# Interleaving the forward and inverse FFT stages of neighbouring channel chunks

## Chip, cores, metric

Each run used one core of one Trainium2 chip. The experiments were spread over three chips (e1 to e6, e7 to e10, e11 and e12), each time with the kernel before run beside them in the same rounds. The metric is device microseconds of one execution; a time is the median of several runs. Every ratio below is the mean time of one kernel's fast runs over the mean of the fast runs of the kernel before in the same rounds, so it is not quite the ratio of the medians.

## The reference

The kernel computes two independent things and puts them side by side in the output: (A) a dilated sliding-window attention over 2048 positions, and (B) an S4 state-space layer, which builds a convolution kernel K per channel and convolves the input u with it by FFT. Only the second half of (B) matters here:

```python
Kf = rfft(pad(K))             # 640 channels, length 2048 padded to 4096
Uf = rfft(pad(u))
y  = irfft(Uf * Kf)[:2048]    # to bfloat16
y  = y + u * Dskip
```

## The kernel before

The program has three stages: tables and K on VectorE (to 405 us), the FFT part (405 to 622 us), and attention (622 to 836 us). The FFT part treats 640 channels in five chunks of 128. Each FFT is two matmul steps. Forward: f1 (with the constant BD1) and f2 (with Tsb). Then VectorE multiplies the spectra (six products, "prod"). Inverse: ia (with EA) and ib (with HB). Every step ends in a tile in PSUM, the memory that the matmuls write (a one-bank tile is 128x512 float32 in these traces), and is copied out ("evacuated") by ScalarE or VectorE.

```python
def fft_chunk(...):                       # cut to its order
    for sig in range(2):                  # K, then U
        for jp in range(8):               # f1: 16 one-bank tiles
            ps = psp.tile([128, 2, 64, 4], f32, tag="bank")
            ...                           # 4 matmuls
            ev(A1[...], ps)
    for b0 in range(0, 32, 2):            # f2: 16 one-bank tiles
        ...                               # 8 matmuls, lhsT=Tsb, rhs=A1
        ev(S[...], ps)
    # prod: Yr = Kr*Ur - Ki*Ui (3 ops), Yi = Kr*Ui + Ki*Ur (3 ops), on VectorE
    for jp in range(8):                   # ia: 8 tiles, lhsT=Y
        ...
        ev(Z[...], ps)
    for lb in range(4):                   # ib: 4 tiles, lhsT=HB, rhs=Z
        ...
        ev(ysb[...], ps)
    ud = u * Dskip; ud = ud + ysb         # VectorE
    for g in range(4):                    # output
        (nc.sync if g % 2 == 0 else nc.scalar).dma_start(out=dst[g, ...], in_=ud[...])

# constants
nc.gpsimd.memset(Tsb[:], 0.0)             # then two loads of Tsb
nc.gpsimd.memset(HB[:], 0.0)              # then four loads of HB
...
ev = Evac(nc, "ad")                       # a = ScalarE, d = VectorE, in turn
for c in range(NCH):
    fft_chunk(tc, pools, C, c, ...)
```

A1, S, Y and Z each have one buffer; PSUM has eight one-bank buffers. A scheduler decides the final order on each engine, close to the program's.

## Time and profile before

| | before |
|---|---|
| time, median of 6 first runs | 837.46 us |
| FFT part: f2 of chunk 0 starts | 446.9 us |
| products of chunks 0 to 4 start | 457.3, 491.9, 526.1, 560.3, 594.4 us |
| attention's first load issued | 622.0 us |
| attention, to the end of the span | 214.0 us |

The distance between the starts of the products of neighbouring chunks (the "pitch") is the measure of the FFT loop: 34.3 us on average here.

First the page's busy rows of the kernel before: each digit is the busy share of one fortieth of the span in tenths; PEclk is the granted TensorE clock in tenths.

```profile
PE   4100000801702603504514768667728989378895
DVE  0899899999999999995113666676623076998670
ACT  1444200100200200200112334243214545202322
PEclk9999999855855855755756778898778999668998
```

The FFT part is slices 20 to 30. No engine is busy throughout, so something serial bounds it. The waits view of the kernel before for 404 to 640 us names it (columns: who waited on whom; total us, times, longest):

```profile
PE ps_ia L283 <- DVE Yf L272: 27.6, 5, 5.5
...
PE ps_f L261 <- DMA Tsb<-c_T: 20.3, 1, 20.3
...
PE ps_f L261 <- ACT A L232: 13.2, 4, 3.4
```

TensorE waits 5.5 us per chunk for the real half of the products, 20.3 us once for the load of Tsb, and about 3.3 us per chunk for the last evacuation of A1. The timeline of POOL in the kernel before shows where the late Tsb comes from (start, length, instruction):

```profile
407.05 10.38 POOL L213 MEMSET Tsb<- 128x12288 bf16 x1
417.33 13.79 POOL L218 MEMSET HB<- 128x16384 bf16 x1
431.03 2.21 POOL L215 DMA_DIRECT2D Tsb<-c_T  x1
433.21 2.19 POOL L216 DMA_DIRECT2D Tsb<-c_T  x1
```

The two memsets stand one after the other before the loads are issued. The ScalarE timeline of the kernel before shows where the A1 wait comes from:

```profile
474.99 2.54 ACT L232 CAST A<-ps_f 128x512 bf16<-128x512 f32 x5 [0.61 <-PE ps_f L252]
477.05 3.43 ACTq L299 DMA_DIRECT2D out_dram<-ud  x2
480.52 1.56 ACT L232 CAST A<-ps_f 128x512 bf16<-128x512 f32 x3 [2.99 <-DVE A L234]
```

ScalarE spends 3.43 us issuing two output DMAs; three A1 evacuations of the next chunk stand behind it. Finally two steady chunks in the windows view (busy us of PE, weight loads, DVE, ACT, POOL, then clock, DMA share, GB/s):

```profile
492.00:526.00 34.00, 24.00 (x448) 22.40 (x448) 23.38 (x30) 12.61 (x22) 0.00 (x0) 0.85 0.16 17
526.00:560.00 34.00, 23.98 (x448) 22.25 (x448) 23.36 (x30) 12.61 (x22) 0.00 (x0) 0.85 0.16 17
```

### The profile page before, as it was taken

Reading aid. Unit: us, or ns where it says so; the run is one execution under the profiler, and the core shown is the slowest. Engines: PE = TensorE matmul, PEld = TensorE weight load, DVE = VectorE, ACT = ScalarE, POOL = GpSimd, SP = SyncE. Lnnn points to the kernel's source line nnn. Section 1 sums busy time; section 2 is a strip of 40 time slices with the busy share of each in tenths; the row PEclk is TensorE's granted clock in tenths of the full one; section 3 lists DMA queues with packets and bytes.
Section 4 is the critical chain, followed back from the end, with each engine's and each line's share of the span. In section 5 each row is a group of like instructions: output and inputs, shape, how many; then the busy total and the mean of one; then the engine's idle time right before and its main releaser. Section 6 shows DMA issues by size and latency. Waiting matters only on the chain.

```text
span 836.0 us, 14737 instructions
## 1 busy us (share of the span) xinstructions
PE 394.8 (47%) x6720; PEld 296.6 (35%) x6720; DVE 597.6 (71%) x567; ACT 192.3 (23%) x327; POOL 39.4 (5%) x33
## 2 busy tenths in 40 slices
PE   4100000801702603504514768667728989378895
PEld 2000000701602503404414657656615466133534
DVE  0899899999999999995113666676623076998670
ACT  1444200100200200200112334243214545202322
POOL 0000000000000000000583000000000000000000
PEclk9999999855855855755756778898778999668998
DMA  4000000000000000000799012021049200000101
GB/s 84 1 0 0 0 0 0 3 0 0 3 0 1 2 0 1 2 0 2 109 58 97 12 17 28 2 27 19 9 82 302 45 2 5 1 0 1 64 1 65
DMA packets 96077, 21.86 MB, mean 26 GB/s; under 512 B 89488, under 2 KB 95888, under 8 KB 95888
## 3 DMA queue, kind: packets, MB, share of 16 engines
q0 software_dynamic: 29184, 2.82, 13.4%
q1 hardware_dynamic: 35552, 9.59, 6.0%
q10 hardware_dynamic: 31280, 8.52, 5.1%
q8 instruction: 52, 0.85, 0.4%
q14 instruction: 9, 0.07, 0.0%
HBM read 18.45 MB, written 5.24 MB: 28 GB/s over the span
## 4 chain that ended last, share of the span: by engine, by line
DVE 49%; PE 30%; DMA 7%; issue 4%; POOL 3%; ACT 3%; ACTq 2%; POOLq 0%; SPq 0%; DVEq 0%
DVE krtmp L139 6%; DVE krtmp L136 5%; DVE Ytab L140 4%; DVE Ytab L137 4%; DVE Ytab L135 4%; DVE Ytab L138 4%; PE ps_o L420 4%; PE ps_op L432 3%; PE ps_qk L354 3%; DVE chsq L123 3%; PE ps_k L169 2%; PE ps_ia L284 2%; PE ps_v L370 2%; DMA wsb<-in_A_wqkv_dram 2%; DVE Xtab L140 2%
## 5 line engine op out<-in xcount | busy, mean ns | idle before, releaser
L168 PE MATMUL ps_k<-Ytab,Xtab 128*32 128x64 bf16 x640 | 50.8, 331 | 260.3 <-DVE Ytab L137 143.6
L168 PEld LDWEIGHTS <-Xtab 128*32 128x32 bf16 x640 | 43.1, 160 | 261.4 <-issue 261.4
L176 ACT CAST Kall<-ps_k 128x512 bf16<-128x512 f32 x20 | 11.8, 588 | 292.2 <-PE ps_k L175 292.2
L384 DVE TENSOR_TENSOR prod<-qT,kT 128x5120 bf16<-128x5120 bf16 x16 | 44.3, 2821 | 37.1 <-ACT qT L362 33.8
L169 PE MATMUL ps_k<-Ytab,Xtab 128*32 128x64 bf16 x640 | 50.2, 327 | 29.5 <-DVE Ytab L140 29.5
L169 PEld LDWEIGHTS <-Xtab 128*32 128x32 bf16 x640 | 44.1, 162 | 33.6 <-DVE Ytab L140 30.8
L261 PE MATMUL ps_f<-A,Tsb 128*128 128x128 bf16 x160 | 39.1, 244 | 33.5 <-DMA Tsb<-c_T 20.3
L418 DVE TENSOR_TENSOR prod<-v,attn 128x2560 bf16<-128x2560 bf16 x32 | 45.9, 1488 | 7.4 <-PE ps_o L420 7.1
L283 PE MATMUL ps_ia<-EA,Yf 128*32 128x256 bf16 x320 | 37.0, 370 | 27.6 <-DVE Yf L272 27.6
L234 DVE CAST A<-ps_f 128x512 bf16<-128x512 f32 x40 | 25.0, 680 | 34.2 <-ACT A L232 25.3
L420 PE MATMUL ps_o<-prod,ident 128*128 128x512 bf16 x160 | 44.1, 410 | 6.5 <-DVE prod L418 5.7
L234 DVE CAST S<-ps_f 128x512 bf16<-128x512 f32 x40 | 25.4, 683 | 24.6 <-PE ps_f L264 24.4
L262 PE MATMUL ps_f<-A,Tsb 128*128 128x128 bf16 x160 | 39.1, 244 | 0.0
L264 PE MATMUL ps_f<-A,Tsb 128*128 128x128 bf16 x160 | 39.0, 244 | 0.0
L263 PE MATMUL ps_f<-A,Tsb 128*128 128x128 bf16 x160 | 39.0, 244 | 0.0
L174 PE MATMUL ps_k<-Ytab,Xtab 64*32 64x64 bf16 x640 | 38.2, 289 | 0.0
L175 PE MATMUL ps_k<-Ytab,Xtab 64*32 64x64 bf16 x640 | 37.8, 286 | 0.0
L432 PE MATMUL ps_op<-wo,o 32*128 32x320 bf16 x640 | 36.8, 298 | 1.8 <-ACT ob L437 1.6
L283 PEld LDWEIGHTS <-Yf 128*32 128x32 bf16 x320 | 23.9, 163 | 30.3 <-DVE Yf L272 28.4
L135 DVE TENSOR_TENSOR Ytab<-Ytab,gY 128x192 bf16<-128x192 bf16 (+4 forms) x25 | 32.3, 1291 | 2.2 <-ACT Ytab L154 2.2
L232 ACT CAST S<-ps_f 128x512 bf16<-128x512 f32 x40 | 23.5, 587 | 43.0 <-PE ps_f L264 43.0
L139 DVE TENSOR_TENSOR krtmp<-Ytab,gY 128x192 bf16<-128x192 bf16 (+4 forms) x25 | 32.4, 1298 | 0.9
(123 smaller groups left out, 1103.2 us busy)
## 6 DMA issues: line engine op xcount, KB each, us to landing
wsb<-in_A_wqkv_dram SPq DMA_DIRECT2D x2, 800.0 KB, 20.9
wo<-in_A_wo_dram ACTq DMA_DIRECT2D x2, 800.0 KB, 17.6
wo<-in_A_wo_dram SPq DMA_DIRECT2D x2, 800.0 KB, 24.8
Tsb<-c_T POOLq DMA_DIRECT2D x2, 768.0 KB, 12.4
Usb<-in_B_u_dram ACTq DMA_DIRECT2D x2, 640.0 KB, 12.4
Usb<-in_B_u_dram SPq DMA_DIRECT2D x2, 640.0 KB, 14.0
out_dram<-ud SPq DMA_DIRECT2D x10, 128.0 KB, 5.2
out_dram<-ud ACTq DMA_DIRECT2D x10, 128.0 KB, 6.5
```

The lines of the kernel that those rows point to most:

```text
L135: V.tensor_tensor(out=Or, in0=Yr, in1=gr, op=A.mult)
L136: V.tensor_tensor(out=t, in0=Yi, in1=gi, op=A.mult)
L139: V.tensor_tensor(out=t, in0=Yr, in1=gi, op=A.mult)
L140: V.tensor_tensor(out=Oi, in0=Oi, in1=t, op=(A.subtract if conj else A.add))
L168: nc.tensor.matmul(o, lhsT=Xtab[:, 0, :, colA], rhs=Ytab[:, 0, :, colA], start=(jj == 0 and dd == 0), stop=False, tile_position=(0, 32 * g ...
L169: nc.tensor.matmul(o, lhsT=Xtab[:, 1, :, colA], rhs=Ytab[:, 1, :, colA], start=False, stop=False, tile_position=(0, 32 * g), skip_group_ch ...
L234: self.nc.vector.tensor_copy(out=out, in_=in_)
L283: MM(o, lhsT=Y[:, :, 0, 4 * j + g], rhs=C["EA"][:, 0, :], start=(jj == 0), stop=False, skip_group_check=True, tile_position=(0, 32 * g))
L384: V.tensor_tensor(out=pr[:], in0=q4[:, :, :, 256 * hf:256 * hf + 256], in1=k4[:, :, :, 256 * hf:256 * hf + 256], op=A.mult)
L418: V.tensor_tensor(out=p2[:], in0=v2[:, 10 * dh:10 * dh + 10, off:off + 256], in1=at[:, w, :].unsqueeze(1).to_broadcast([128, 10, 256]), op ...
L420: MM(ops[b][:].rearrange("p a b -> p (a b)"), lhsT=ident[:], rhs=p2[:, 2 * b:2 * b + 2, :].rearrange("p a b -> p (a b)"), start=(w == 0), ...
L432: MM(pst[sc][eh][:], lhsT=o2[32 * sc:32 * sc + 32, d, 128 * q:128 * q + 128], rhs=wo2[32 * sc:32 * sc + 32, d, 320 * eh:320 * eh + 320], s ...
```

## The change

The intent is to fill TensorE's idle time in one chunk with matmuls of its neighbour. The parts:

1. Each chunk is cut into units: 17 forward (8 f1, 8 f2, prod) and 7 inverse (4 ia, 2 ib, output). The forward units of chunk c+1 are interleaved evenly with the inverse units of chunk c.
2. PSUM tiles grow to two banks (four buffers), so there are half as many evacuations, each twice as wide; two of three go to ScalarE ("aad").
3. The Tsb memset moves to VectorE, half of the HB memset to ScalarE.
4. U is transformed before K; Y gets two buffers; pools are rearranged so that `base` is freed before the FFT part.

```diff
-    nc.gpsimd.memset(Tsb[:], 0.0)
+    nc.vector.memset(Tsb[:], 0.0)
...
-    nc.gpsimd.memset(HB[:], 0.0)
+    nc.gpsimd.memset(HB[:, 0:64, :], 0.0)
+    nc.scalar.memzero(HB[:, 64:128, :])
...
-def fft_chunk(tc, pools, C, c, Usb, Ksb, Dsb, out_b, ev):
+def fft_units(tc, pools, C, c, Usb, Ksb, Dsb, out_b, ev):
...
+            ps = psp.tile([128, 4, 64, 4], f32, name="ps_f1", tag="bank2")   # two banks
...
+    for sig in (1, 0):
+        for jq in range(4):
+            fwd.append(f1(sig, jq))
+    for b0 in range(0, 32, 4):
+        fwd.append(f2(b0))
+    fwd.append(prod)
+    for jq in range(4):
+        inv.append(ia(jq))
+    for lb in range(2):
+        inv.append(ib(lb))
+    inv.append(fin)
...
+def interleave(a, b):                  # spreads b evenly among a
...
-            ev = Evac(nc, "ad")
-            for c in range(NCH):
-                fft_chunk(tc, pools, C, c, Usb, Kall[:, c], Dsb, out_b, ev)
+    ev = Evac(nc, "aad")
+    prev_inv = []
+    for c in range(NCH):
+        fwd, inv = fft_units(tc, pools, C, c, Usb, Kall[:, c], Dsb, out_b, ev)
+        interleave(fwd, prev_inv)
+        prev_inv = inv
+    interleave(prev_inv, [])
```

## The prediction

> **What bounds the kernel now.** The 40-slice view has three stages: table generation bound by VectorE (to about 405 us), the FFT part (405 to 622), attention (622 to 836). The change touches only the middle; the instruction order of the first and last stage is the same.
>
> In the FFT part the timeline shows:
> - Start-up: Tsb memset on POOL 407.1-417.4, HB memset 417.4-431.1, then Tsb load issued 431, landed 446.7. Both f1 halves were done by 428, so f2 of chunk 0 waits 20.3 us for Tsb (waits view).
> - Five serial chunks of 34.1 us (f2 starts 446.9, about 482, 516, 550, 585): f2 about 9.5, the six products on VectorE 7.1 with TensorE idle 5.5, ia about 6.5, ib about 4, f1 about 8, of which about 3 is ScalarE issuing two output DMAs (3.4 us) ahead of the last A1 evacuations.
> - Granted clock 0.85 in those chunks: f2 starts cold (16 matmuls per 1.65 us) and warms (0.895). The Trainium skill, "TensorE: Matmul & The Clock Gate", Part 1, states half rate after an idle window of some 3.4 us; this trace agrees.
> - Tail: last ud 613.4, output DMA landed 621.6, attention starts.
>
> **Costs of the change.**
> 1. Memsets: HB half stays on POOL (13.8/2 = 6.9 us), HB half on ScalarE as 4096 words (slope of its copies, 0.59 us for 512 and 1.80 for 1920: about 3.6 us), Tsb on VectorE as 6144 words (estimate 6.4 us at one element per cycle, the skill's "VectorE: DVE Perf Modes", zero memsets as uint32). POOL is free to issue at 414 rather than 431. But one HB load now stands before Tsb, U's loads on ScalarE wait for its memset, U is still loading until about 425 and shares the DMA engines, and U's f1 now comes first. I expect Tsb landed about 435, A1 ready about 435: f2 of chunk 0 ends about 446 instead of 456. Gain about 10 us.
> 2. Evacuations of two banks: VectorE 2x0.68 becomes 1.21, ScalarE 2x0.59 becomes 1.01. 22 per chunk, two thirds on ScalarE: no engine's bound (VectorE about 19 us, ScalarE about 18-19 with DMA issue, TensorE about 17 warm).
> 3. Interleave. The TensorE order shows what it really is: after f2 of chunk c comes only one f1 group, then a matmul of ia(c), which needs the products of c. TensorE is in order, so the product wait (4.6 us to Yr, 7.1 to Yi) stays mostly exposed and the clock still falls. In three of four boundaries ScalarE issues the two output DMAs (3.4 us) just before the last S evacuation, delaying the products. What overlaps well is f1+ia and f2+ib. By hand from these durations: about 26.5 us (boundary 0-1), 30.5, 27, 30.5. Sum 115 against 4x34.1 = 136: gain about 20 us.
> 4. The last inverse runs alone: about 32 us from its f2 end to the landed output, as now; loss 0 to 4.
>
> Attention unchanged at about 214 us. 837.5 - 10 - 20 = about 807 us, range 790 to 822. Faster by over 2% (under 820.7): 0.84; within 2%: 0.15; slower: 0.01.
>
> **Signs.** Right if: Tsb lands 430-440; f2-to-f2 pitch 26-31 us; TensorE still waits over 4 us on VectorE's Yf once per chunk; ScalarE's output DMA issue stands before the S evacuation in three boundaries; first stage and attention lengths unchanged within 2 us.
>
> **What would make it wrong.** Slower: HB and U loads crowd out Tsb; VectorE's in-order queue (ud, products) holds evacuations and the four 2-bank buffers run out. Faster: f1+ia and f2+ib stay warm and the pitch falls near 22 us (then about 785).

## The result

812.55 us (median of 8 runs, 810.14 to 815.05) against 837.82 us (16 runs): ratio 0.9695, 95% interval 0.9677 to 0.9712.

The page's busy rows of the changed kernel:

```profile
PE   4100000710710800800815758767528899379895
DVE  0899899999999999999132665665521186997770
ACT  1443300010010010010024436535205446012222
PEclk9999999965755755855858879879659999578998
```

They look much as before, only shorter. The waits view of the changed kernel, same columns and window as before:

```profile
PE ps_ia L299 <- DVE Yf L284: 35.5, 5, 8.7
...
PE ps_f L269 <- DMA Tsb<-c_T: 8.5, 1, 8.5
```

Software pipelining was meant to hide the wait for the products, but that wait has grown, from 27.6 to 35.5 us. What fell is the Tsb wait, by 11.8 us; the A1 waits of 13.2 us (which were on ScalarE) are down to about 2. POOL in the changed kernel:

```profile
407.06 6.96 POOL L218 MEMSET HB<- 128x8192 bf16 x1
414.32 1.63 POOL L222 DMA_DIRECT2D HB<-c_HB  x1 [0.30 <-POOL HB L218]
415.94 2.17 POOL L215 DMA_DIRECT2D Tsb<-c_T  x1
425.67 2.16 POOL L216 DMA_DIRECT2D Tsb<-c_T  x1 [7.55 <-issue]
```

The first Tsb load is issued 15 us earlier. The second had to wait 7.55 us at its issue and is only 7.5 us earlier, so f2 starts at 437.0 instead of 446.9. ScalarE and then VectorE in the changed kernel, at the end of f2 of chunk 1, show why the product wait grew:

```profile
472.14 1.01 ACT L233 CAST S<-ps_f 128x1024 bf16<-128x1024 f32 x1 [0.78 <-PE ps_f L272]
472.65 3.44 ACTq L324 DMA_DIRECT2D out_dram<-ud  x2
476.13 1.01 ACT L233 CAST S<-ps_f 128x1024 bf16<-128x1024 f32 x1 [2.97 <-issue]
```

```profile
473.71 1.22 DVE L235 CAST A<-ps_f 128x1024 bf16<-128x1024 f32 x1
477.17 1.23 DVE L282 TENSOR_TENSOR Yf<-S 128x2048 bf16<-128x2048 bf16 x1 [2.25 <-ACT S L233]
478.32 1.22 DVE L283 TENSOR_TENSOR pt<-S 128x2048 bf16<-128x2048 bf16 x1
```

The interleave moved the output DMAs of chunk 0 just ahead of the last S evacuation of chunk 1. That evacuation waits 2.97 us for ScalarE's issue, VectorE waits for it, and TensorE waits for VectorE. Two chunks in the windows view of the changed kernel:

```profile
447.00:477.00 30.00, 21.88 (x448) 20.03 (x448) 17.87 (x15) 14.21 (x15) 0.00 (x0) 0.89 0.09 10
477.00:505.00 28.00, 21.99 (x448) 19.79 (x448) 17.83 (x15) 14.20 (x15) 0.00 (x0) 0.82 0.11 12
```

The same 448 matmuls take 28 to 30 us instead of 34. VectorE's busy time fell from 23.4 to 17.9 us per chunk, but nothing is near full.

The spans add up as follows, from the last f2 matmul of each chunk (before: 456.3, 490.8, 525.0, 559.2, 593.4; after: 445.4, 472.8, 503.5, 531.1, 561.7):

| part of the span | before | after | gain |
|---|---|---|---|
| to the end of f2 of chunk 0 | 456.3 | 445.4 | 10.9 |
| four pitches of f2 ends | 34.5, 34.2, 34.2, 34.2 | 27.4, 30.7, 27.6, 30.6 | 20.8 |
| last f2 to attention's first load | 28.6 | 34.5 | -5.9 |
| attention | 214.0 | 213.8 | 0.2 |
| span | 836.0 | 810.0 | 26.0 |

### The profile page after: what moved, and what is told of

It is laid out like the page before. It is cut to its first block, busy times and chain, and to the rows that moved or that the text cites. A ratio compares the mean times of both kernels' runs of the same rounds, so it can differ in the third digit from the quotient of the medians.

```text
span 810.0 us, 14618 instructions
## 1 busy us (share of the span) xinstructions
PE 383.9 (47%) x6720; PEld 283.7 (35%) x6720; DVE 575.4 (71%) x494; ACT 205.3 (25%) x292; POOL 22.4 (3%) x32
## 5 line engine op out<-in xcount | busy, mean ns | idle before, releaser
L176 ACT CAST Kall<-ps_k 128x512 bf16<-128x512 f32 x20 | 11.8, 588 | 292.3 <-PE ps_k L175 292.3
L452 DVE TENSOR_TENSOR prod<-qT,kT 128x5120 bf16<-128x5120 bf16 x16 | 44.3, 2821 | 37.3 <-ACT qT L430 33.9
L299 PE MATMUL ps_ia<-EA,Yf 128*32 128x256 bf16 x320 | 31.0, 353 | 35.5 <-DVE Yf L284 35.5
L233 ACT CAST A<-ps_f 128x1024 bf16<-128x1024 f32 x29 | 28.5, 1023 | 47.8 <-PE ps_f L256 44.6
L269 PE MATMUL ps_f<-A,Tsb 128*128 128x128 bf16 x160 | 35.6, 223 | 10.4 <-DMA Tsb<-c_T 8.5
L235 DVE CAST S<-ps_f 128x1024 bf16<-128x1024 f32 x14 | 17.1, 1223 | 27.7 <-PE ps_f L272 27.5
L270 PE MATMUL ps_f<-A,Tsb 128*128 128x128 bf16 x160 | 35.7, 223 | 0.0
L271 PE MATMUL ps_f<-A,Tsb 128*128 128x128 bf16 x160 | 35.6, 223 | 0.0
L272 PE MATMUL ps_f<-A,Tsb 128*128 128x128 bf16 x160 | 35.6, 223 | 0.0
L299 PEld LDWEIGHTS <-Yf 128*32 128x32 bf16 x320 | 20.7, 172 | 39.5 <-DVE Yf L284 36.4
L233 ACT CAST S<-ps_f 128x1024 bf16<-128x1024 f32 x26 | 25.7, 1014 | 31.0 <-PE ps_f L272 19.1
```

The source lines that it names most:

```text
L233: self.nc.scalar.copy(out=out, in_=in_)
L269: MM(ps[:, kk, 0], lhsT=T[:, 3 * a, :], rhs=rr, start=(kk % 2 == 0), stop=False, skip_group_check=True)
L270: MM(ps[:, kk, 1], lhsT=T[:, 3 * a, :], rhs=ri, start=False, stop=False, skip_group_check=True)
L299: MM(o, lhsT=Y[:, :, 0, 4 * j + g], rhs=C["EA"][:, 0, :], start=(jj % 2 == 0), stop=False, skip_group_check=True, tile_position=(0, 32 * g))
L452: V.tensor_tensor(out=pr[:], in0=q4[:, :, :, 256 * hf:256 * hf + 256], in1=k4[:, :, :, 256 * hf:256 * hf + 256], op=A.mult)
```

## The experiments

Twelve more kernels were run. The table has, for each, the time, the ratio to the kernel before, and from its profile the moment at which the FFT part ends (attention's first load is issued), the mean pitch between the starts of the products, and the length of the attention. The last three columns are read from one profiled execution of each kernel; how much they vary between executions was not measured.

| kernel | time us | ratio (95%) | FFT ends | pitch | attention |
|---|---|---|---|---|---|
| before | 837.8 | 1 | 622.0 | 34.3 | 214.0 |
| changed | 812.6 | 0.9695 (0.9677-0.9712) | 596.3 | 29.8 | 213.8 |
| e1 memsets only | 827.9 | 0.9888 (0.9860-0.9917) | 611.2 | 34.2 | 214.0 |
| e2 serial | 845.2 | 1.0073 (1.0023-1.0124) | 625.0 | 37.3 | 221.5 |
| e8 serial, alternating | 844.5 | 1.0081 (1.0051-1.0111) | 621.6 | 36.5 | 221.0 |
| e3 output on SyncE | 801.3 | 0.9572 (0.9546-0.9597) | 585.8 | 27.6 | 213.6 |
| e4 late inverse | 809.1 | 0.9661 (0.9638-0.9685) | 593.2 | 29.4 | 213.8 |
| e5 = e4 + e3 | 806.6 | 0.9631 (0.9604-0.9658) | 590.9 | 28.5 | 215.6 |
| e7 = e5, A1 on ScalarE | 794.5 | 0.9482 (0.9453-0.9512) | 579.0 | 25.5 | 213.4 |
| e6 POOL free | 808.4 | 0.9657 (0.9629-0.9684) | 592.1 | 29.3 | 214.1 |
| e9 = e7 + e6 | 794.5 | 0.9479 (0.9429-0.9529) | 574.7 | 25.9 | 221.1 |
| e10 = e3 + e6 | 800.9 | 0.9560 (0.9509-0.9610) | 583.0 | 27.5 | 218.9 |
| e11 one-bank tiles | 818.9 | 0.9787 (0.9727-0.9848) | 600.9 | 31.3 | 213.8 |
| e12 = e7, one-bank | 801.0 | 0.9555 (0.9508-0.9602) | 583.0 | 27.9 | 212.6 |

**A caution on the last column.** The attention took 212.6 to 215.6 us in most profiles and 218.9 to 221.5 us in four (e2, e8, e9, e10). In the builds compared (the changed kernel, e2, e7, e9) its instructions stand in the same order on TensorE, VectorE and ScalarE. The windows view of the changed kernel and then of e9, first 20 us of the attention and the rest, shows what differs:

```profile
596.20:616.20 20.00, 11.47 (x98) 8.82 (x99) 6.82 (x10) 6.55 (x13) 0.41 (x2) 0.73 1.05 304
616.20:810.00 193.80, 156.28 (x1704) 82.57 (x1701) 117.22 (x58) 63.94 (x121) 0.50 (x7) 0.88 0.10 27
```

```profile
574.70:594.70 20.00, 10.96 (x90) 8.03 (x92) 6.72 (x10) 5.58 (x11) 0.41 (x2) 0.67 1.04 303
594.70:795.80 201.10, 163.41 (x1705) 90.58 (x1709) 117.21 (x58) 64.93 (x122) 0.50 (x7) 0.86 0.10 26
```

The granted clock is lower in e9 (0.67 against 0.73, 0.86 against 0.88) and TensorE is busy 7.1 us longer for the same matmuls in the long part (163.4 against 156.3). The Trainium skill, "TensorE: Matmul & The Clock Gate", section "Part 1: The HAM clock gate", says that the activity window is free-running; that the start of the attention falls differently on it would fit, but no run here shows that as the cause. The individual times of e9 (797.55, 789.91, 797.61, 791.48), of e10 (803.70, 796.75, 798.06, 805.03) and of e2 (848.59, 841.02, 848.41, 841.93) also fall in two groups, some 7 us apart, and the profiled execution was of the longer one each time. So effects inside the FFT part are read from the FFT end and the pitch, and total times of kernels within 8 us of each other are compared with care.

### e1: the memsets alone

```diff
 (kernel before)
-    nc.gpsimd.memset(Tsb[:], 0.0)
+    nc.vector.memset(Tsb[:], 0.0)
-    nc.gpsimd.memset(HB[:], 0.0)
+    nc.gpsimd.memset(HB[:, 0:64, :], 0.0)
+    nc.scalar.memzero(HB[:, 64:128, :])
```

> The kernel before with only the memsets moved (Tsb to VectorE, half of HB to ScalarE). Theory: f2 of chunk 0 starts at about 437 us instead of 447, the five serial chunks keep their 34.1 us pitch, total 10 us less: 826 to 829 us. Rival (the load of U and the contention on the DMA engines set the start, so that earlier memsets only move the wait): total within 3 us of before.

Measured: 827.9 us; f2 starts at 436.7; pitch 34.2. The theory held: three lines of memset bring 9.9 of the change's 25.3 us, and the start-up gain is independent of the interleave.

### e2 and e8: the change without the interleave

```diff
 (changed kernel)
-        interleave(fwd, prev_inv)
-        prev_inv = inv
-    interleave(prev_inv, [])
+        interleave(fwd, [])
+        interleave(inv, [])
 (e8 only)
-    ev = Evac(nc, "aad")
+    ev = Evac(nc, "ad")
```

> The changed kernel with the interleave taken out (forward then inverse of each chunk in turn), all else of the change kept: split memsets, two-bank evacuations, two thirds of them on ScalarE. Theory (the interleave only overlaps f1 with ia and f2 with ib, while the wait for the products stays exposed): f2-to-f2 pitch about 31-32 us against 29.8, total 815 to 823 us, so the interleave alone is worth only about 3 to 10 of the 25 us. Rival (the interleave is what brings the pitch down from 34.1): pitch 34, total 826 to 832 us.

Measured: 845.2 us and pitch 37.3, outside what either theory expected. I had thought that wider evacuations would help the serial form too; they hurt it. Taking off the longer attention (221.5 - 213.8 = 7.7 us), the interleave is worth 625.0 - 596.3 = 28.7 us in the FFT part, not 3 to 10. That holds with two-bank tiles; e11 below gives it with one-bank tiles, where it is far less.

> e2 (serial, two-bank evacuations) with the evacuations alternating between ScalarE and VectorE as in the kernel before, in place of two in three on ScalarE. It splits why the serial form of the changed kernel (845) is 17 us slower than the kernel before with the memsets moved (828). If the share of ScalarE is the cause: 826 to 832 us. If the two-bank tiles are (half as many, twice as long evacuations at the head and tail of every stage, with nothing beside them): 838 to 847 us. My guess is the second.

Measured: 844.5 us, pitch 36.5, FFT end 621.6. Against e1 (FFT end 611.2), the two-bank tiles together with the other differences that were not separated (U first, two buffers for Y, the pools) cost 10.4 us, and two thirds on ScalarE another 3.4. The guess held by the total, but with help from the attention: with the changed kernel's 213.8 us in place of 221.0 the total would be about 837, just under the guessed 838 to 847 and still well above the 826 to 832 of the other theory. The windows view from products to products, e1 and then e2:

```profile
481.26:515.35 34.09, 23.90 (x448) 22.18 (x448) 23.48 (x31) 12.59 (x22) 0.00 (x0) 0.85 0.16 17
```

```profile
483.80:521.37 37.57, 24.61 (x448) 22.89 (x448) 18.96 (x17) 13.96 (x14) 0.00 (x0) 0.77 0.14 15
```

VectorE does 4.5 us less work in e2, and yet the chunk takes 3.5 us more. Every hand-over between steps is longer, because a step can start only when the last, now twice as wide, evacuation of the step before is done: last ia to first ib 1.7 us instead of 1.2, last f2 to products 1.8 instead of 1.25, first f1 to first f2 8.5 instead of 7.5. The granted clock also falls to 0.77, and f2 itself takes 9.7 instead of 8.5 us. These four differences (0.5, 0.55, 1.0 and 1.2 us) make up 3.25 of the 3.5 us; the first three are the reading that in a serial chain the latency of one evacuation counts, not the throughput of many. What lowers the clock was not tested.

### e3: all output DMAs on SyncE

```diff
 (changed kernel)
-            (nc.sync if g % 2 == 0 else nc.scalar).dma_start(out=dst[g, ...], in_=ud[...])
+            nc.sync.dma_start(out=dst[g, ...], in_=ud[...])
```

> The changed kernel with all four output DMAs of a chunk issued by SyncE. Theory (ScalarE's 3.3 us of DMA issue ahead of the last S evacuation delays the products at three of four chunk ends and before the last inverse): products start about 3 us earlier there, total 802 to 806 us (8 to 10 less, 1 to 2 given back where four issues in a row delay the last output). Rival (VectorE's own queue, with its ud add and S and A1 evacuations, sets the start of the products): no more than 2 us.

Measured: 801.3 us, ratio 0.9572 against 0.9695 (1.3% or about 10 us less). The products start at 446.5, 474.8, 502.3, 529.4 and 556.7 instead of 446.7, 477.2, 505.1, 535.4 and 565.9, and TensorE's wait on Yf falls from 35.5 to 27.2 us, what it was in the kernel before (27.6). The waits view of e3, and its last two S evacuations of the last chunk, which now follow each other without a gap:

```profile
PE ps_ia L299 <- DVE Yf L284: 27.2, 5, 5.9
```

```profile
554.78 1.93 ACT L233 CAST S<-ps_f 128x1024 bf16<-128x1024 f32 x2 [0.78 <-PE ps_f L272]
```

The theory held. What the interleave had added to that wait was thus the DMA issue, and one line takes it away. The Trainium skill, "DMA: Bandwidth & Descriptors", section "Issuing engines are not separate DMA queues", says that using several issuing engines saves only the sequencer's time, "which is usually small relative to the DMA itself". Here it was not small: 3.44 us of issue on ScalarE for two DMAs that took 6.3 us (median) from issue to landing, and on the critical path.

### e4 and e5: the inverse later

```diff
 (changed kernel; e5 also has e3's edit)
-        interleave(fwd, prev_inv)
+        interleave(fwd[:8], [])            # all f1 of the next chunk first
+        interleave(fwd[8:], prev_inv)
```

> The changed kernel with the inverse of chunk c only started after all eight f1 groups of chunk c+1 (f2 then interleaves with ia and ib). Theory (TensorE, in order, stands at ia for the products): TensorE's wait on Yf falls from 35.5 us to 8-14 us (the last inverse still waits), the pitch from 29.8 to 23-26 us, total 785 to 796 us. In the built order the output DMAs also move behind the last S evacuation, so this run holds the effect of e3 at those chunk ends too. Rival (evacuations by ScalarE and VectorE and the four two-bank buffers set the pitch): the wait only moves from Yf to buffer releases, pitch 28-30, total within 4 us of 812.

Measured: 809.1 us, pitch 29.4, 3.4 us less than the changed kernel by the medians (the intervals of the two ratios overlap; the FFT part ends 3.1 us earlier). The first half of my theory held: TensorE's wait on Yf is only 6.0 us, once, at the last inverse. The second half fell: the pitch did not follow. The rival came out right. TensorE's waits in e4:

```profile
PE ps_f L256 <- DVE A L235: 13.7, 6, 4.7
...
PE ps_f L269 <- DVE A L235: 8.4, 2, 6.0
...
PE ps_ia L299 <- DVE Yf L284: 6.0, 1, 6.0
```

and VectorE's timeline in e4 after f2 of chunk 0:

```profile
449.63 1.22 DVE L284 TENSOR_TENSOR Yf<-Yf,pt 128x2048 bf16<-128x2048 bf16 x1
450.77 1.22 DVE L235 CAST A<-ps_f 128x1024 bf16<-128x1024 f32 x1
451.90 1.22 DVE L286 TENSOR_TENSOR pt<-S 128x2048 bf16<-128x2048 bf16 x1
453.03 1.22 DVE L235 CAST A<-ps_f 128x1024 bf16<-128x1024 f32 x1
454.17 1.22 DVE L287 TENSOR_TENSOR Yf<-Yf,pt 128x2048 bf16<-128x2048 bf16 x1
455.30 1.22 DVE L235 CAST A<-ps_f 128x1024 bf16<-128x1024 f32 x1
```

The "aad" pattern gives three of the eight A1 evacuations to VectorE, which is just then busy with the products; they queue among them, the last ends at 456.5, and f2 waits for it. The wait for VectorE has only changed its name.

> e4 and e3 together. Theory: the DMA issue now only stands among the A1 evacuations, which have some slack while the products run, so little more than e4: 0 to 5 us less than e4, 783 to 793 us. Rival (ScalarE is the bound once the wait is gone): 10 us or more less than e4.

Measured: 806.6 us, 2.5 less than e4 (again with overlapping intervals): as far from e4 as expected, but 13.6 us above the expected range, for the same reason. 23.3 us of TensorE's waits are for VectorE's A1. Since e4 also moves the output DMAs, the fair test of the late inverse is e5 against e3, both with the output DMAs on SyncE: the FFT part ends at 590.9 instead of 585.8. So by itself the late inverse gained nothing here: it cost 5.1 us, 1.4 of them before the first f2.

### e7: late inverse, and A1 on ScalarE

```diff
 (e5)
-            ev(A1[:, :, sig, 16 * jq:16 * jq + 16]..., ps)
+            (nc.scalar.copy if c > 0 else ev)(A1[:, :, sig, 16 * jq:16 * jq + 16]..., ps)
-    ev = Evac(nc, "aad")
+    ev = Evac(nc, "da")
```

> e5 (late inverse, output DMAs on SyncE) with the A1 evacuations of chunks 1 to 4 all on ScalarE and all other evacuations alternating. Theory formed from e4's trace (the product wait went, but the A1 evacuations that fell to VectorE stand among the products in its queue, so the next f1 and f2 wait for VectorE instead): pitch falls to 22-24.5 us (eight A1 evacuations of 1.0 us beside the 7.1 us of products, then about 14 us of f2, ia and ib), TensorE's waits on VectorE's A1 go, total 778 to 790 us. Rival (the gain of a late inverse is lost to the colder clock or to four two-bank buffers, whichever engine evacuates): within 6 us of e5's 806.6.

Measured: 794.5 us, ratio 0.9482, pitch 25.5, 12.1 us less than e5; the attention is of the same short length as in the changed kernel. The waits on VectorE's A1 are gone. The run does not separate A1's move from the new order of the other evacuations ("da" for "aad"), and A1 on ScalarE without the late inverse was not tried. It missed the expected numbers by 1 us of pitch and 4.5 us of time; the rest is in e7's waits:

```profile
PE ps_f L269 <- ACT A L257: 12.2, 4, 3.0
...
PE ps_ia L299 <- DVE Yf L284: 6.2, 1, 6.2
```

TensorE still waits 3.0 us per chunk for the last of eight A1 evacuations, which fill ScalarE for 7.4 us beside the 7.1 us of products on VectorE. Both evacuating engines are now full in that stretch, and the wait that is left is one for work, not for order.

### e6, e9 and e10: the start-up

```diff
 (changed kernel; e9: e7, e10: e3 with the same edit)
-    nc.gpsimd.memset(HB[:, 0:64, :], 0.0)
+    nc.vector.memset(HB[:, 0:64, :], 0.0)
```

> The changed kernel with POOL's half of the HB memset moved to VectorE, behind the Tsb memset; in the built order both Tsb loads are then issued before any HB load. Theory (one HB load ahead of Tsb, and the wait of the second Tsb issue, hold f2 of chunk 0 back): Tsb lands at 426-431 us, then A1 (ready at 430) ends the wait, f2 starts at 430-432 instead of 437, total 805 to 808 us. Rival (DMA engines shared with U's load set it): Tsb still lands after 434, total within 3 us of 812.

Measured: 808.4 us; f2 starts at 434.6 instead of 437.0. Both Tsb loads were issued by 417.2, ahead of any HB load, but took 17.4 to 19.5 us to land instead of 11.2 to 16.5. So the order of issue was worth about 2 us of the 6 I expected; the rival is the better description of the start-up, though the total lies just outside the 809 to 815 that it allowed. The FFT part ends 4.2 us earlier; the other 2 us came mostly in the first two pitches, and no run explains them. Nor does the run tell whether the U load is what Tsb shared the DMA engines with.

> e7 with e6's memset placement: the best version so far, if both hold. Theory: e6's 2 to 4 us come on top of e7, as they lie in the start-up alone: 774 to 788 us, 1 to 5 us under e7. Rival (the start-up gain is lost because HB lands later and ib of chunk 0 waits): no less than e7.

> The changed kernel with e3 and e6 together, its interleave untouched. If the two are independent: 801.3 - 4 = 796 to 799 us.

Measured: 794.5 and 800.9 us, no less than e7 and e3; both missed the expected totals. Their FFT parts end 4.3 and 2.8 us earlier than those of e7 and e3 (574.7 against 579.0, 583.0 against 585.8), and the attention of the profiled run is longer by 7.7 and 5.3 us. The times are therefore inconclusive for the total; in the FFT part the start-up gain is there. The two shorter times of each are on average 3.8 us under e7 and 3.9 us under e3, which would fit a gain that the longer attention hides in the other executions, but no shorter one was profiled.

### e11 and e12: one-bank tiles in the interleaved form

```diff
 (e11: changed kernel; e12: e7; the same for f2, ia, ib)
-            ps = psp.tile([128, 4, 64, 4], f32, name="ps_f1", tag="bank2")
+            ps = psp.tile([128, 2, 64, 4], f32, name="ps_f1", tag="bank")
 (PSUM pool: bufs=8 instead of 4; twice as many units)
```

> The changed kernel with one-bank PSUM tiles (eight buffers, half the columns per evacuation, as in the kernel before), all else of the change kept. Two-bank tiles cost the serial form 3.2 us of pitch (34.1 to 37.3 us). If they cost the interleaved form likewise: pitch 26-28 us against 29.8, total 800 to 806. If the neighbouring stage fills what their longer heads and tails leave open, as I expect: pitch 28.5-30, total 805 to 813. The pitch between the starts of the products is the measure, since the attention stage was 7 us longer in some runs at a lower granted clock (213.7 against 221 us).

Measured: 818.9 us, pitch 31.3, FFT end 600.9 with a short attention. Both expectations were missed: one-bank tiles are slower here, by 4.6 us in the FFT part. So two-bank tiles cost about 10 us in the serial form (with the differences that e8 does not separate) and save about 5 in the interleaved one. Read the other way, e1 against e11 gives the interleave with one-bank tiles (and with U first, the pools and two thirds on ScalarE): 611.2 - 600.9 = 10.3 us, against 28.7 with two-bank tiles. Neither is the worth of the interleave by itself; the two parts depend on each other.

> e7 (late inverse, SyncE output DMAs, A1 of chunks 1 to 4 on ScalarE) with one-bank tiles. ScalarE's sixteen A1 evacuations then take about 8.2-9.4 us instead of 7.4, but the heads and tails of the stages shrink by about 0.5 us each: pitch 24.5-26.5 us against e7's 25.5, total 788 to 798 us; no clear difference from e7's 794.5.

Measured: 801.0 us, pitch 27.9, slower than e7 by 2.4 us of pitch and missed too. Sixteen evacuations of 0.59 us sum to 9.4 us, eight of 1.01 us to 8.1, and once the stages overlap it may be the sum that counts. That this is the whole reason was not tested.

## Why the prediction was right

The time (812.6 against 807, range 790 to 822) and the direction were right. Point by point:

- **Start-up, predicted -10 us:** measured -10.9 at the end of f2 of chunk 0, and e1 confirms that the memsets alone do it. That the sum is so close is partly luck, as two errors cancelled: Tsb was in place at 437.0, not 435, also because of the 7.55 us that the second Tsb load waited at its issue, which I did not foresee; and f2 then took 8.4 us, not the 11 of 435 to 446. A third error cost nothing: I thought that U's loads on ScalarE would wait for its memset, but they were issued at 405.14 and 405.82 while the memset ran (405.5 to 409.1), and f2 waited for Tsb alone.
- **Interleave, predicted -20 us, pitches 26.5, 30.5, 27, 30.5:** measured -20.8, pitches 27.4, 30.7, 27.6, 30.6. The reason was right too: TensorE keeps its order and meets ia(c) one f1 group after f2(c), so the wait for the products stays exposed (35.5 us), and at three of the four later chunk ends (1, 3 and 4, the last inverse), as predicted, the output DMAs on ScalarE stand ahead of the last S evacuation. e3 shows the second point by taking it away; e4 shows the first.
- **The term that was mis-sized: the last inverse,** "about 32 us ... as now; loss 0 to 4". The kernel before took 28.6 us, not 32, and the changed one 34.5: a loss of 5.9. That is about the whole distance between 807 and 812.6. The last chunk, too, has two output DMAs on ScalarE ahead of its last S evacuation:

```profile
561.52 3.27 ACTq L324 DMA_DIRECT2D out_dram<-ud  x2
564.83 1.01 ACT L233 CAST S<-ps_f 128x1024 bf16<-128x1024 f32 x1 [2.81 <-issue]
```

It also has one more VectorE operation (ud) among its products. In e3, where both are gone from there, the same stretch takes 30.4 us (555.4 to 585.8): 4.1 of the 5.9 us went with them. The rest was not separated.

- **What I did not see: the value of the parts.** I had taken the wider evacuations for neutral. e8 shows that they, with the differences not separated from them, cost the serial form 10 us, and e11 that they pay only once stages overlap, so that the interleave is worth about 29 us in the FFT part with these tiles, partly to pay for them, and about 10 with one-bank tiles.
- **The clock,** where I cited the skill's page "TensorE: Matmul & The Clock Gate": f2 of chunk 0 in the kernel before ran at 1.70 us per 16 matmuls while the clock was at 0.50 and at 0.895 at full clock, as that page states. The mean clock in the interleaved chunks stayed at 0.82 to 0.89, about the 0.85 of before: long waits for the products remain (7.1 us per chunk on average).

## What to carry to other kernels

Interleaving two iterations in program order hides a wait only if enough independent work stands *between* the producer and the consumer on the in-order engine: here one group of matmuls stood before a wait of 8.7 us, and even with eight groups there nothing was gained (with the output DMAs on SyncE in both, 5.1 us were lost) until the evacuations of those groups were taken off the engine that produces the awaited result. After reordering, look at what else moved: the output DMAs slid in front of a critical evacuation and cost 10 us, a one-line fix. The wider evacuation, with what came with it, cost about 10 us in the serial chain and saved about 5 in the overlapped one, so its width should be chosen after the overlap, not before.

## What the Trainium skill lacked or had wrong

- "VectorE: DVE Perf Modes", section "Zero memsets can be issued as uint32 (trn2)": it says one cycle per element, which at the 0.96 GHz of the page's specifications is 6.4 us for 6144 words (an estimate from that page). The trace's row is 5.18 us long, but that does not show the page wrong: in e6, e9 and e10 a second VectorE memset, of 4096 words, follows, and the ends of the two rows lie 4.27 us apart although the second row is only 3.47 us long. 4.27 us is what the page's rate gives for 4096 words (an estimate from it), so the row of a memset may well begin late; no run here settles it.
- "DMA: Bandwidth & Descriptors", section "Issuing engines are not separate DMA queues": it calls the issue time usually small. Two output DMAs of 128 KB each took 3.44 us to issue on ScalarE, more than half of the 6.3 us to landing, and the next evacuation stood still for 2.97 us; moving them to SyncE saved about 10 us (e3).
- "TensorE: Matmul & The Clock Gate", section "Part 1: The HAM clock gate", puts the ramp penalty under 1% of a typical span. Here the attention, with the same instruction order, took 212.6 to 215.6 us in most profiles and 218.9 to 221.5 in four: e2's was 7.7 us longer than the changed kernel's, 0.9% of its span. That does not contradict the page, and no run shows that the ramp is its cause; but it is as large as most effects studied here.
